# A fused window-attention and gated-FFN kernel: longer warm-up matmuls, one tile in two token parts, one copy on the vector engine, earlier final waits, and one add on GpSimd

## Chip, cores and metric

The kernel runs on one NeuronCore of one Trainium2 chip. The metric is the device time of one execution in microseconds (us), the median of several. The profile's span (first to last recorded instruction) is 1.7 to 2.4 us shorter than that time.

Names used: PE is the matmul engine, PEld its weight loads, DVE the vector engine, ACT the scalar engine, POOL GpSimd, SP SyncE, which here only issues transfers. A "q" after a name (POOLq) is that engine's instruction sequencer. "ps" is PSUM.

## The reference, cut to what matters

```python
def reference(A_x, A_wqkv, A_wo, B_x, B_w_gate, B_w_up, B_w_down):
    x = A_x                                   # 1 x 2048 x 576, bf16
    xn = layernorm(x)
    s = window_attention(xn, A_wqkv, A_wo)    # 32 heads of 18, each query sees the last 256 keys
    h = sigmoid(xn @ B_w_gate) * (xn @ B_w_up)   # 576 -> 4608
    return x + s * silu(h @ B_w_down)         # B_x is not used
```

## The kernel before

The 2048 tokens go through in four chunks of 512. The program is a graph of operations that a list scheduler, inside the kernel, puts in order for each engine before anything is emitted. A change in one place can therefore move instructions elsewhere. These are the parts that the change touches (cuts are marked):

```python
NWARM = 60
PARTS = ((0, 1), (1, 2), (2, 4))      # token blocks of 128 in which gate/up tiles 0-2 of chunk 0 are computed

# build_consts: matmuls on zeros, which keep PE active until the first real work is there
zero = self.hT[:, 0, 0:2 * P]                        # 256 columns
z = op("DVE", 600, lambda e: e.memset(zero, 0.0), "init:zero", prio=0)
...
for i in range(NWARM):                               # each is a pair of 64-row matmuls
    ... pair(eng, self.halves(h, 2 * P), lambda r, t: zero[r, 0:P], lambda r, t: zero[r, :], True, True)

# build_ln, chunk 0: the first 64 columns of the normalised row are written twice
dup = op("POOL", 260, lambda e, ...: e.tensor_scalar(self.xnr[:, sn, 0:RD], x_in[:, 0:RD], ..., ALU.subtract, ALU.mult), ...)

# attention: spreading the queries to the padded layout, 160 transfers issued by GpSimd
o = self.dma(dst, src, ..., f"dma:sp:{c}:{u}:{w}:{gi}", ("qk", par, gi), deps=[ev, war, self.op_qz], prio=1, eng="POOL")

# build_final: the last steps of a token block (t = tanh part, s_ = attention, xf = x)
q2 = op("DVE", ..., lambda e: e.scalar_tensor_tensor(t, t, 1.0, s_, ALU.add, ALU.mult), ...)
q3 = op("DVE", dve_ns(w, 2.0), lambda e: e.tensor_tensor(xf, xf, t, ALU.add), f"fq3:{nm}", deps=[q2, o_dx], prio=2)
# then: out[rows] <- xf, from SyncE. The last block is done in 384 + 192 columns, with one store.

# run_engine: after its last store SyncE waits for every transfer lane
if e == "SP":
    for i, n in enumerate(lane_cnt):
        if n > 0:
            eng.wait_ge(lanes[i], n)
    eng.nop()
...
with nc.Block() as block:             # each engine's program; all meet at the block's end
```

The softmax here doesn't subtract the row's maximum and nothing guards it: scores larger than these inputs give would overflow.

## Time and profile before

| | before |
|---|---|
| time, median of the first 3 runs | 579.93 us (579.84 to 580.57) |
| span of the profile | 578.4 us |
| first real gate/up matmul starts | 8.49 us |
| tile 3 (first full-width tile) starts | 16.49 us |
| last matmul starts | 573.51 us |
| last store issued, seen landed | 575.26, 577.05 us |

First the page's table of busy times (busy us, share of the span, instructions), and its summary of the chain that ended last:

```profile
PE 569.9 (99%) x9542; PEld 362.2 (63%) x9542; DVE 345.5 (60%) x837; ACT 267.8 (46%) x379; POOL 179.9 (31%) x290
...
PE 97%; DVE 2%; issue 1%; ACT 0%; POOL 0%; DVEq 0%
```

PE is all that matters between the first real matmul and the last; only the two ends are open to a change like this one. The timeline of the start (columns: start us, duration us, engine, source line, operation, output<-input, shape, count, and in brackets the idle time before it and what ended it):

```profile
5.03 0.74 POOL L500 TENSOR_SCALAR xnr<-x,small 128x64 bf16<-128x64 bf16 x1
...
5.91 0.32 PE L550 MATMUL ps<-ident,xnr 64*128 64x64 bf16 x10
...
9.31 0.43 DVE L493 TENSOR_SCALAR xnr<-x,small 128x576 bf16<-128x576 bf16 x1 [0.85 <-POOL small L488]
9.38 0.73 POOL L500 TENSOR_SCALAR xnr<-x,small 128x64 bf16<-128x64 bf16 x1
...
10.26 0.32 PE L550 MATMUL ps<-ident,xnr 64*128 64x64 bf16 x10 [0.16 <-DVE small L465]
...
12.73 0.21 PE L98 MATMUL ps<-xnT,wgs 64*128 64x128 bf16 x1 [0.92 <-issue]
...
16.49 0.39 PE L98 MATMUL ps<-xnT,wgr 64*128 64x512 bf16 x2
```

L550 is a transpose of a normalised block. The first and the last of them wait for GpSimd's copy (L500, 0.73 us). For the last the view names a memset of the vector engine (L465) instead; in the code no transpose depends on it, and the copy had ended at 10.11, shortly before. At 12.73 one matmul comes 0.92 us late ("issue": it waits for nothing that the profile shows); from the start of the one ahead of it, at 11.60, to its own it is 1.14 us.

The tail, from the same view:

```profile
573.67 0.36 DVE L1004 TENSOR_TENSOR xf<-xf,thf 128x384 bf16<-128x384 bf16 x1
...
573.95 0.60 DVE L994 TENSOR_TENSOR s_attn<-s_attn,ps 128x96 bf16<-128x96 bf16 x2
...
574.98 0.26 DVE L1004 TENSOR_TENSOR xf<-xf,thf 128x192 bf16<-128x192 bf16 x1
575.26 0.34 SPq L254 DMA_DIRECT2D out_dram<-xf  x1
```

The last view: the instructions that belong to two source lines, the final wait loop (L1151) and the block (L1154). Its columns are line, sequencer, operation, count, shortest/median/longest duration in ns, first and last start in us:

```profile
L1151 SPq EVENT_SEMAPHORE  x28: 17/28/28, 575.7 to 577.9; - x28
```

SyncE's 28 waits start some 61 ns apart, with one gap at the lane of the last store: 15 of them come only after it has landed.

### The profile page before, as it was taken

How to read it: one execution, taken by the hardware profiler on the slowest of the kernel's cores; microseconds unless marked ns; L12 is line 12 of the kernel's file. 1: busy time of each engine (PE TensorE's matmuls, PEld its weight loads, DVE VectorE, ACT ScalarE, POOL GpSimd, SP SyncE). 2: the span in 40 equal slices, each digit the busy share in tenths (PEclk: the TensorE clock that was granted, in tenths of full speed). 3: DMA queues.
4: the chain of work that ended last, by engine and by line, in shares of the span. 5: the costliest groups of instructions: out<-in, count | busy, mean ns of one | idle time of the engine just before them, and what ended most of it. 6: DMA issues, size and time to landing. Idle time of an engine off the chain costs nothing.

```text
span 578.4 us, 21485 instructions
## 1 busy us (share of the span) xinstructions
PE 569.9 (99%) x9542; PEld 362.2 (63%) x9542; DVE 345.5 (60%) x837; ACT 267.8 (46%) x379; POOL 179.9 (31%) x290
## 2 busy tenths in 40 slices
PE   8999999999999999999999999999999999999996
PEld 7555455678985556555788875555457754444786
DVE  4478989845899775577876578877321133333123
ACT  2247568421676653856663566685221023232111
POOL 7466454107564443145534354340000000000000
PEclk9999999999999999999999999999999999999999
DMA  8978865922313433333611023343340015442010
GB/s 241 272 200 202 223 188 159 213 46 55 90 51 95 133 94 110 93 92 96 116 36 43 19 57 105 108 119 111 114 144 22 23 58 152 132 141 74 2 43 23
DMA packets 104908, 62.06 MB, mean 107 GB/s; under 512 B 15308, under 2 KB 103452, under 8 KB 104816
## 3 DMA queue, kind: packets, MB, share of 16 engines
q1 hardware_dynamic: 99696, 55.95, 35.4%
q0 software_dynamic: 5120, 4.74, 3.3%
q8 instruction: 75, 1.23, 0.9%
q14 instruction: 17, 0.14, 0.1%
HBM read 51.61 MB, written 2.36 MB: 93 GB/s over the span
## 4 chain that ended last, share of the span: by engine, by line
PE 97%; DVE 2%; issue 1%; ACT 0%; POOL 0%; DVEq 0%
PE ps L98 96%; DVE hT L890 1%; PE ps L550 1%; ACT tring L887 0%; DVE pvs L767 0%; DVE s_attn L994 0%; DVE thf L999 0%; DVE xf L1004 0%; POOL small L488 0%; DVE expr L714 0%; DVE xnr L493 0%; DVE small L465 0%; DVE pvs L771 0%; DVE hT L418 0%; DVE small L486 0%
## 5 line engine op out<-in xcount | busy, mean ns | idle before, releaser
L98 PE MATMUL ps<-xnT,wgs 64*128 64x512 bf16 (+2 forms) x2400 | 288.4, 368 | 1.0 <-issue 0.9
L98 PEld LDWEIGHTS ps<-xnT,wgs 64*128 64x128 bf16 x2400 | 111.7, 94 | 113.7 <-PE ps L98 1.6
L701 ACT ACTIVATE expr<-ps 128x1024 bf16<-128x1024 f32 (+2 forms) x160 | 156.2, 983 | 52.1 <-PE ps L98 51.6
L98 PE MATMUL ps<-wd_sb,hT 64*128 64x288 bf16 (+2 forms) x2448 | 154.9, 276 | 0.0
L887 ACT ACTIVATE tring<-ps 128x512 bf16<-128x512 f32 x144 | 85.7, 596 | 130.4 <-PE ps L98 128.0
L890 DVE SCALAR_TENSOR_TENSOR hT<-tring,ps 128x512 bf16<-128x512 bf16 x144 | 98.5, 685 | 79.4 <-ACT tring L887 77.3
L98 PEld LDWEIGHTS ps<-wd_sb,hT 64*128 64x128 bf16 x2448 | 118.0, 94 | 22.3
L254 POOL DMA_DIRECT2D qk<-qd x160 | 82.2, 523 | 86.6 <-DVE qd L588 48.7
L666 POOL TENSOR_SCALAR kx<-kprev,small 128x256 bf16<-128x256 bf16 x64 | 64.8, 1023 | 72.1 <-PE ps L98 71.7
L714 DVE TENSOR_TENSOR expr<-expr,mask 128x256 bf16<-128x256 bf16 (+2 forms) x232 | 64.9, 301 | 29.8 <-ACT expr L701 28.4
L767 DVE TENSOR_REDUCE pvs<-ps 64x304 f32<-64x608 f32 x64 | 50.4, 787 | 17.5 <-PE ps L98 16.3
L98 PE MATMUL ps<-qk,kx 64*128 64x320 bf16 (+4 forms) x736 | 59.9, 251 | 0.0
L98 PE MATMUL ps<-xnT,wgr 64*128 64x512 bf16 (+2 forms) x300 | 55.9, 368 | 1.4 <-DVE hT L890 1.2
L98 PEld LDWEIGHTS ps<-qk,kx 64*128 64x128 bf16 x736 | 31.7, 94 | 25.2 <-ACT expr L701 1.7
L984 ACT ACTIVATE thf<-ps 128x576 bf16<-128x576 f32 (+3 forms) x22 | 11.4, 519 | 70.1 <-PE ps L98 69.5
L98 PEld LDWEIGHTS ps<-v_aug,expr 64*128 64x128 bf16 x2432 | 35.5, 93 | 6.2 <-issue 0.2
L98 PE MATMUL ps<-v_aug,expr 64*128 64x19 bf16 (+1 forms) x2432 | 35.9, 170 | 0.0
L98 PE MATMUL ps<-xnT,wqk 64*128 64x512 bf16 x256 | 32.0, 376 | 0.0
L588 DVE CAST qd<-ps 128x1024 bf16<-128x1024 f32 (+1 forms) x20 | 22.1, 1116 | 7.7 <-PE ps L98 7.5
L666 DVE TENSOR_SCALAR kx<-qk,small 128x512 bf16<-128x512 bf16 x64 | 23.5, 388 | 5.3 <-DMA qk<-qd 4.6
L987 DVE SCALAR_TENSOR_TENSOR thf<-thf,ps 128x576 bf16<-128x576 bf16 x12 | 9.1, 754 | 29.3 <-ACT thf L984 28.7
L98 PEld LDWEIGHTS ps<-xnT,wgr 64*128 64x128 bf16 x300 | 14.9, 94 | 15.4 <-DVE hT L890 3.4
(66 smaller groups left out, 293.8 us busy)
## 6 DMA issues: line engine op xcount, KB each, us to landing
wgs<-in_B_w_gate_dram SPq DMA_DIRECT2D x72, 256.0 KB, 3.1
wgs<-in_B_w_up_dram SPq DMA_DIRECT2D x72, 256.0 KB, 3.5
wd_sb<-in_B_w_down_dram SPq DMA_DIRECT2D x9, 576.0 KB, 4.9
qk<-qd POOLq DMA_DIRECT2D x100, 36.0 KB, 2.0
xf<-in_A_x_dram SPq DMA_DIRECT2D x16, 144.0 KB, 2.8
out_dram<-xf SPq DMA_DIRECT2D x16, 144.0 KB, 1.8
xr<-in_A_x_dram SPq DMA_DIRECT2D x6, 288.0 KB, 3.8
wqk<-in_A_wqkv_dram SPq DMA_DIRECT2D x2, 576.0 KB, 6.6
```

The costliest lines, as they stand in the source:

```text
L98: res = eng.matmul(outs[i], lhs(ROWS[t], i), rhs(ROWS[t], i), start=start, stop=stop, tile_position=(64 * t, 0))
L254: o = self.op(eng, DMA_ISSUE_NS[eng], lambda e: e.dma_start(dst, src), name, deps, prio, nbytes=nbytes)
L550: res = eng.transpose(self.psb[:, o:o + 64], src(r, k * P), self.ident[r, :], tile_position=(64 * t, 0))
L588: return eng.tensor_copy(dst, self.both(h, n))
L666: return e.tensor_scalar(self.kx[:, sx, pos:pos + n_ // SW, t, :], src.rearrange("p (s k) -> p s k", k=SW), self.half[:, t:t + 1], None, A ...
L701: return eng.activation(self.expr[:, se, :, lo * SW:NT], self.both(h, NT)[:, :, lo * SW:NT], ACTF.Exp, scale=SM_SCALE)
L714: return eng.tensor_tensor(e_, e_, m_, ALU.mult)
L767: return eng.tensor_reduce(out[ROWS[i]], src, mybir.AxisListType.X, ALU.add)
L887: th = op("ACT", act_ns(NT), lambda e: e.activation(self.tring[:, st, :], bank(h, 0), ACTF.Tanh, scale=0.5), f"th:{c}:{ft}", deps=[pg, dt_ ...
L890: mu = op("DVE", dve_ns(NT), lambda e: e.scalar_tensor_tensor(self.hT[:, ft, :], self.tring[:, st, :], 1.0, bank(h, 1), ALU.add, ALU.mult) ...
L984: return e.activation(v2(t)[:, a:b, :], y2()[:, a:b, :], ACTF.Tanh, scale=0.25)
L987: q1 = op("DVE", dve_ns(w), lambda e: e.scalar_tensor_tensor(v2(t), v2(t), 1.0, y2(), ALU.add, ALU.mult), f"fq1:{nm}", deps=[th, f2], prio=0)
```

## The change

The intent: warm-ups of the full 512 columns, so that fewer instructions keep PE as active; the early gate/up tiles done one after the other, with tile 2 in two token parts and not three; the copy of 64 columns on the vector engine; SyncE's waits in its idle time ahead of the last store; and the 384-column add of the last block off the vector engine, which has the tail's chain to itself then.

```diff
-NWARM = 60
-PARTS = ((0, 1), (1, 2), (2, 4))
+NWARM = 36
+PARTS = (((0, 1), (1, 2), (2, 4)), ((0, 1), (1, 2), (2, 4)), ((0, 2), (2, 4)))
...
-        zero = self.hT[:, 0, 0:2 * P]
+        zero = self.hT[:, 0, :]
...
-                return pair(eng, self.halves(h, 2 * P), ...)
-            w = op("PE", 220 if i < 18 else 110, f_warm, ...)
+                return pair(eng, self.halves(h, NT), ...)
+            w = op("PE", 432 if i < 9 else 216, f_warm, ...)
... # layer-norm of chunk 0: the copy goes from POOL's tensor_scalar to DVE's tensor_copy
... # early tiles: loop over tiles outside, over their parts inside
-        q3 = op("DVE", dve_ns(w, 2.0), lambda e: e.tensor_tensor(xf, xf, t, ALU.add), f"fq3:{nm}", deps=[q2, o_dx], prio=2)
+        big = w < D and c0 == 0
+        q3 = op("POOL" if big else "DVE", 700 if big else dve_ns(w, 2.0), lambda e: e.tensor_tensor(xf, xf, t, ALU.add), f"fq3:{nm}",
+                deps=[q2, o_dx], prio=2)
...
+                if e == "SP" and o is self.prog[e][-1]:
+                    for i, n in enumerate(lane_cnt):
+                        if n > 0 and i not in outs:
+                            eng.wait_ge(lanes[i], n)
...
             if e == "SP":
-                for i, n in enumerate(lane_cnt):
-                    if n > 0:
-                        eng.wait_ge(lanes[i], n)
+                for i in outs:
+                    eng.wait_ge(lanes[i], lane_cnt[i])
                 eng.nop()
```

`big` is true for one operation only, the add of the first 384 columns of the last token block.

More of the change, by code (lines that the diff above doesn't have):

```diff
@@ L55 @@
 NTAIL = 96
-NWARM = 60
-PARTS = ((0, 1), (1, 2), (2, 4))
+NWARM = 36
+PARTS = (((0, 1), (1, 2), (2, 4)), ((0, 1), (1, 2), (2, 4)), ((0, 2), (2, 4)))
+XPRIO = 0
 NQK = 5
@@ L381, in load_x @@
             for i in range(BPC):
-                self.x_dma[i] = (self.dma(self.x0[:, i, :], self.x[i * P:(i + 1) * P, :], P * D * 2, f"dma:x{i}", ("x0", i), prio=0),
+                self.x_dma[i] = (self.dma(self.x0[:, i, :], self.x[i * P:(i + 1) * P, :], P * D * 2, f"dma:x{i}", ("x0", i), prio=XPRIO * (i > 1)),
                                  self.x0[:, i, :])
@@ L424, in f_warm @@
             def f_warm(eng):
-                return pair(eng, self.halves(h, 2 * P), lambda r, t: zero[r, 0:P], lambda r, t: zero[r, :], True, True)
-            w = op("PE", 220 if i < 18 else 110, f_warm, f"warm:{i}", deps=[z], prio=4, acq=None if i else h, odeps=[w])
+                return pair(eng, self.halves(h, NT), lambda r, t: zero[r, 0:P], lambda r, t: zero[r, :], True, True)
+            w = op("PE", 432 if i < 9 else 216, f_warm, f"warm:{i}", deps=[z], prio=4, acq=None if i else h, odeps=[w])
             w.filler = h
@@ L495, in build_ln @@
                 ALU.subtract, ALU.mult), f"ln:ap:{st}", deps=[rs, ag, dn], prio=pr)
-            if c:
-                dup = op("DVE", 180, lambda e, sn=sn: e.tensor_copy(self.xnr[:, sn, 0:RD], self.xnr[:, sn, RD:2 * RD]),
-                         f"ln:dup:{st}", deps=[ap], prio=pr)
-            else:
-                dup = op("POOL", 260, lambda e, ss=ss, x_in=x_in, sn=sn: e.tensor_scalar(
-                    self.xnr[:, sn, 0:RD], x_in[:, 0:RD], self.mv[:, ss, 0:1], self.rstd[:, ss, :],
-                    ALU.subtract, ALU.mult), f"ln:dup:{st}", deps=[rs, ag, dn], prio=pr)
+            dup = op("DVE", 180, lambda e, sn=sn: e.tensor_copy(self.xnr[:, sn, 0:RD], self.xnr[:, sn, RD:2 * RD]),
+                     f"ln:dup:{st}", deps=[ap], prio=pr)
             if c:
@@ L505, in build_ln @@
             self.r_st.release(ss, ap)
-            self.r_st.release(ss, dup)
             if c:
@@ L869, in gate_up @@
             sw, fc = slots[ft // WG], slice((ft % WG) * P, (ft % WG + 1) * P)
-            b0, b1 = (0, BPC) if part is None else PARTS[part]
+            b0, b1 = (0, BPC) if part is None else PARTS[ft][part]
             t0, n = b0 * P, (b1 - b0) * P
@@ L901, in build_ffn @@
             hs = [self.pool_f.hold() for _ in range(2)] + [self.pool_s.hold()]
-            his = [None] * early
-            for part in range(len(PARTS)):
-                los = [gate_up(ft, hs[ft], 0, None if part else hs[ft], part, [his[ft]]) for ft in range(early)]
-                for ft in range(early):
-                    u = his[ft] = gate_up(ft, hs[ft], 1, None, part, [los[ft]])
-                    if part == len(PARTS) - 1:
-                        tail(ft, hs[ft], u)
-                    if part == len(PARTS) - 1 and ft == 1:
-                        self.r_w.release(slots[0], u)
+            for ft, h in enumerate(hs):
+                u = None
+                for part in range(len(PARTS[ft])):
+                    lo = gate_up(ft, h, 0, None if part else h, part, [u])
+                    u = gate_up(ft, h, 1, None, part, [lo])
+                tail(ft, h, u)
+                if ft == 1:
+                    self.r_w.release(slots[0], u)
         for ft in range(early, NFT):
@@ L1127, in emit @@
                     o.tok = (("E", e), cnt[e])
+        outs = [i for lane, i in self.lane_ids.items() if lane[0] == "out"]
         def semof(key):
```

## The prediction

> **What bounds the kernel.** TensorE. The table of busy times has PE at 569.9 of 578.4 us (99%), and the chain of work that ended last is 97% PE. From 12.7 us to 573.7 us PE has only a dozen gaps of 0.2 to 0.9 us. So nothing can be won in the middle; the change works on the first 16.5 us and on what follows the last matmul (573.7 us).
>
> **The start (timeline, 0 to 17 us).** The first real matmuls wait for layer-norm, then the transposes. Before: 24 pairs of 256-column warm-ups until 5.8, transpose 0 at 5.91, first gate matmul at 8.49. PE then idles twice: 0.3 us at 9.9 (transpose 3 waits for GpSimd's copy, 0.73 us, ended 10.11), and 1.1 us at 11.6, where a matmul that waits for no semaphore comes late. I read this second one as the instruction stream: an instruction packet of 16 KB starts at 10.33 in the DMA records, and PE resumes at 12.73 with its 450th instruction.
>
> After:
> - Warm-ups are 15 + 7 + 3 pairs of 512 columns. Cold pairs cost 427 ns (2 x 213 measured), warm ones 218 (2 x 109). The clock rose 3.8 us after the first warm-up, which agrees with about 3.4 us in the Trainium skill ("TensorE: Matmul & The Clock Gate", Part 1). The first block then ends near 6.4, not 5.8; first gate matmul near 8.9: +0.4 us.
> - The copy moves to DVE (about 0.1 us): transpose 3 no longer waits: -0.3.
> - PE issues 80 fewer instructions before the gates and longer ones after, so the 450th comes near 14.5 while its packet should be there by 14.2: -1.0 to -1.1.
> - Waiting for the last transpose's evictions may cost 0.2 again; tile 2 in two parts saves 0.03 of matmul time.
>
> Net: tile 3's first matmul moves from 16.49 to about 15.4-15.6: -1.0 us (my range -1.3 to -0.1). Weights for later tiles land 3 us or more ahead of use, so the gain should last.
>
> **The end.** The last store is issued at 575.26 and has landed by 577.05. The list of SyncE instructions shows 29 semaphore waits after its issue, 61 ns each; 13 are hidden in the flight, but 15 stand after the out lane's wait and end at 578.0. Put ahead of the store they fall into SyncE's idle time (570.4 to 575.2): -0.9 to -1.0 us.
>
> The 384-column add leaves DVE (0.36 us at 573.67), so the tail's first multiply can start about 0.18 us earlier. On GpSimd it takes an estimated 0.9 us (2.6 cycles per element, "GPSIMD Engine Reference", section 3.1, plus start-up; here a 256-column copy takes 0.43), ending near 574.7, ahead of DVE's last add (575.05). It may slow DVE's last operations: -0.1 (range -0.2 to +0.3).
>
> **Middle.** The scheduler reorders some rows; work is equal: 0 +- 0.5 us.
>
> **Sum.** -1.0 - 0.95 - 0.1 = -2.1 us: **577.8 us**, 8-in-10 range 576.7 to 579.2. Faster by over 2%: 0.005; within 2%: 0.99; slower: 0.005.
>
> **Right or wrong by:** the first gate matmul at about 8.9; no PE gap near 11.6; tile 3 at about 15.5; 29 waits before the last store, and about 1.0 us (not 2.0) less between landing and end; GpSimd's add 0.7 to 1.1 us, off the chain.
>
> **What would make it wrong:** the instruction stall only moves, to where PE is again ahead of its packet; warm-ups of 512 columns shift the clock's rise; GpSimd's add becomes the last thing the store waits for; new gaps in the middle from the changed order, which can each be 0.3 to 0.9 us.

## More of the kernel before

```profile
L1154 POOLq DRAIN  x1: 8982/8982/8982, 389.6 to 389.6; - x1
L1154 PEldq DRAIN  x1: 658/658/658, 573.1 to 573.1; - x1
L1154 ACTq DRAIN  x1: 281/281/281, 574.2 to 574.2; - x1
L1154 DVEq DRAIN  x1: 297/297/297, 575.0 to 575.0; - x1
...
L1154 SPq DRAIN  x1: 13/13/13, 578.2 to 578.2; - x1
```

The DRAIN lines are each engine's own end of the block. GpSimd's is 8.98 us long and starts at 389.6 us, because GpSimd has nothing left to do from there on. It costs nothing there, and it is counted in no engine's busy time.

## The result, and the profile after

The changed kernel is slower: 583.92 us (583.38 to 584.12, 4 runs), before 580.25 us (579.84 to 580.60, 4 runs). The ratio is 1.0062 (95% interval 1.0045 to 1.0079). Ratios here and below are the mean time of one kernel's fast runs over that of the other's in the same rounds, so not quite the ratio of the medians quoted. The outputs are correct.

Busy times and chain after:

```profile
PE 569.1 (98%) x9484; PEld 351.3 (60%) x9484; DVE 346.7 (60%) x840; ACT 268.8 (46%) x379; POOL 175.6 (30%) x287
...
PE 96%; DVE 1%; ACT 1%; issue 1%; DVEq 0%
```

PE does a little less and the span is 3.4 us longer, so time is added where PE stands still. It is not at the start:

```profile
6.13 0.31 PE L545 MATMUL ps<-ident,xnr 64*128 64x64 bf16 x10
...
9.33 1.12 DVE L494 TENSOR_SCALAR xnr<-x,small 128x576 bf16<-128x576 bf16 x1 [0.23 <-PE ps L99]
9.36 0.93 POOL L451 MEMSET v_aug<- 128x192 bf16 x1
...
11.19 0.32 PE L545 MATMUL ps<-ident,xnr 64*128 64x64 bf16 x10
...
12.31 0.28 PE L99 MATMUL ps<-xnT,wgr 64*128 64x256 bf16 x2
...
15.50 0.38 PE L99 MATMUL ps<-xnT,wgr 64*128 64x512 bf16 x2
```

Tile 3 starts at 15.50, as predicted; the late matmul of before is gone. (The vector engine's normalisation of the last block took 1.12 us here, where it took 0.43 before. It ran beside a GpSimd memset. PE was not ready for that block any sooner, so this did no harm.)

The tail is better too:

```profile
572.09 0.91 POOL L999 TENSOR_TENSOR xf<-xf,thf 128x384 bf16<-128x384 bf16 x1 [189.54 <-DVE thf L993]
...
572.18 0.61 DVE L988 TENSOR_TENSOR s_attn<-s_attn,ps 128x96 bf16<-128x96 bf16 x2 [0.18 <-PE ps L99]
...
573.24 0.26 DVE L999 TENSOR_TENSOR xf<-xf,thf 128x192 bf16<-128x192 bf16 x1
573.59 0.34 SPq L255 DMA_DIRECT2D out_dram<-xf  x1
```

The store is issued 1.67 us earlier than before, and GpSimd's add is over (573.00) before the vector engine's last one begins. The loss is behind it. The waits of SyncE in the last 12 us (who waited for whom, us in total, times, longest):

```profile
SPq L1155 <- PEq L1155: 6.2, 1, 6.2
SPq L1146 <- POOL xf L999: 2.6, 1, 2.6
SPq L1153 <- DMA out_dram<-xf: 1.4, 1, 1.4
SPq L1146 <- DVE xf L999: 0.5, 1, 0.5
```

(L1146 is the wait for what the last store needs: it waits for GpSimd's add, and then 0.5 us more for the vector engine's.)

The instructions of the moved waits (L1136), of the wait for the last store (L1153) and of the block (L1155), with columns as before, one fence each:

```profile
L1136 SPq EVENT_SEMAPHORE  x27: 17/28/28, 568.8 to 570.4; - x27
```

```profile
L1153 SPq EVENT_SEMAPHORE  x1: 17/17/17, 575.4 to 575.4; - x1
```

```profile
L1155 POOLq EVENT_SEMAPHORE  x2: 17/17/17, 581.6 to 581.7; - x2
...
L1155 POOLq DRAIN  x1: 9532/9532/9532, 572.0 to 572.0; - x1
...
L1155 SPq DRAIN  x1: 13/13/13, 575.6 to 575.6; - x1
L1155 SPq EVENT_SEMAPHORE  x1: 17/17/17, 581.7 to 581.7; - x1
```

The 27 waits are in SyncE's idle time now. SyncE is done at 575.6 and then stands for 6.2 us at the block's meeting point. The first line names PEq as the releaser; this is the case that the view's own warning is about, for PE had been done for 9 us. The one that came last is GpSimd: its DRAIN runs from 572.04 to 581.58. The add that keeps GpSimd busy until 573.00 has moved the start of that drain from 389.6 to 572.0, and nothing hides it there. The chain of work that ended last does not show this either: it ends with the vector engine's last add, since a drain is not counted as work.

The two spans add up as follows, in us. In the row "landed to the end", 1.37 is the rest of SyncE's waits and the meeting of the engines, and 6.42 is the drain with the meeting behind it.

| stretch | before | after | difference |
|---|---|---|---|
| start to tile 3 | 16.49 | 15.50 | -0.99 |
| tile 3 to the last matmul | 557.02 | 556.44 | -0.58 |
| last matmul to the last store's issue | 1.75 | 1.65 | -0.10 |
| issue to landed, as SyncE sees it | 1.79 | 1.79 | 0 |
| landed to the end | 1.37 | 6.42 | +5.05 |
| span | 578.42 | 581.80 | +3.38 |

### The profile page after: what moved, and what is told of

Its sections match the earlier page's. It is cut to its first block, busy times and chain, and to the rows that moved or that the text cites. A ratio compares the mean times of both kernels' runs of the same rounds, so it can differ in the third digit from the quotient of the medians.

```text
span 581.8 us, 21366 instructions
## 1 busy us (share of the span) xinstructions
PE 569.1 (98%) x9484; PEld 351.3 (60%) x9484; DVE 346.7 (60%) x840; ACT 268.8 (46%) x379; POOL 175.6 (30%) x287
## 3 DMA queue, kind: packets, MB, share of 16 engines
q0 software_dynamic: 5120, 4.74, 3.3%
## 4 chain that ended last, share of the span: by engine, by line
PE 96%; DVE 1%; ACT 1%; issue 1%; DVEq 0%
PE ps L99 96%; DVE hT L885 1%; PE ps L545 1%; ACT tring L882 0%; ACT expr L696 0%; ACT xnT L522 0%; DVE s_attn L988 0%; DVE thf L993 0%; DVE hT L419 0%; DVE xf L999 0%; DVE small L487 0%; DVE small L410 0%; DVE expr L709 0%; DVEq L1146 0%
## 5 line engine op out<-in xcount | busy, mean ns | idle before, releaser
L99 PEld LDWEIGHTS ps<-wd_sb,hT 64*128 64x128 bf16 x2448 | 112.5, 94 | 27.3
L661 POOL TENSOR_SCALAR kx<-kprev,small 128x256 bf16<-128x256 bf16 x64 | 63.4, 999 | 53.0 <-PE ps L99 52.3
```

What stands on the lines that cost most here:

```text
L99: res = eng.matmul(outs[i], lhs(ROWS[t], i), rhs(ROWS[t], i), start=start, stop=stop, tile_position=(64 * t, 0))
L661: return e.tensor_scalar(self.kx[:, sx, pos:pos + n_ // SW, t, :], src.rearrange("p (s k) -> p s k", k=SW), self.half[:, t:t + 1], None, A ...
```

## The experiments

Theory A: the loss is GpSimd's drain, which begins after its last instruction. Rival B: it is the new order of work or the lower mean clock (0.994 against 1.0). Rival C: it is the store's wait for the slow add.

### e1_add_on_dve, e2_only_add, e3_after_no_drain, e4_late_memset

e1 is the changed kernel with the add back on the vector engine. e2 is the kernel before with the add alone moved. e3 is the changed kernel whose block is told to end without GpSimd's drain. e4 is the kernel before with a late GpSimd instruction that nobody waits for.

```diff
# e1, on the changed kernel
-        big = w < D and c0 == 0
+        big = False
# e2, on the kernel before: the q3/big lines of the change, nothing else
# e3, on the changed kernel
-        with nc.Block() as block:
+        with nc.Block(no_gpsimd_drain=True) as block:
# e4, on the kernel before, after q3
+        if w < D and c0 == 0:
+            op("POOL", 150, lambda e: e.memset(self.kprev[:, 0, 0:64], 0.0), "late", deps=[q2, list(self.op_kp.values())], prio=9)
```

> The changed kernel with its last 384-column add put back on the vector engine, all else kept. Theory A (the GpSimd drain at the block's end, 9.5 us long, now starts at 572.0 and is the last thing to end): the drain goes back to about 390 us, the span ends with SyncE's wait near 575.6 plus 0.2, so about 575.9 span and 577.3 to 577.8 us measured, 2.3 to 3.0 us under the kernel before. Rival B (the loss comes from the new order of work or from the lower mean clock, 0.994): stays within 1 us of 583.9.

> The kernel before with only the 384-column add moved to GpSimd. Theory A: GpSimd's last instruction starts at 573.7, its drain ends about 9.5 us later at 583.2, the span is about 583.4 (before 578.4) and the time about 585.2, 5 us slower than before. Rival B: within 0.5 us of before. Rival C (the store waits for a slow GpSimd add): at most 0.5 us slower, and the store issued later than 575.3.

> The changed kernel, add on GpSimd, but the block closes without GpSimd's drain. Theory A: no long GpSimd DRAIN in the trace, end about 0.2 us after SyncE's last wait at 575.4, span about 575.7, time 577.2 to 577.7. Rival B: stays at about 583.9. Result must stay correct.

> The kernel before plus one small GpSimd memset (64 columns of a buffer nobody reads any more) after the last block's product, near 573.7; nothing waits for it. Theory A: any late GpSimd instruction exposes the drain: ends about 9 us after it, near 582.7 to 583.2, about 4.5 to 5 us slower than before. Rival C (only the add counts, since the store waits for it): no change, within 0.3 us.

| run | time, us (range) | ratio to before (95%) | landed to end, us |
|---|---|---|---|
| before | 580.61 (579.92 to 581.18) | | 1.37 |
| e1 | 578.19 (577.95 to 578.44) | 0.9959 (0.9944 to 0.9974) | 0.46 |
| e2 | 585.61 (585.21 to 586.44) | 1.0089 (1.0074 to 1.0104) | 6.43 |
| e3 | 579.01 (577.67 to 579.68) | 0.9970 (0.9954 to 0.9987) | 0.52 |
| e4 | 584.86 (583.91 to 587.67) | 1.0086 (1.0055 to 1.0117) | 5.58 |

GpSimd's drain in the instructions of the block, first e1, then e2, then e4:

```profile
L1155 POOLq DRAIN  x1: 8969/8969/8969, 382.6 to 382.6; - x1
```

```profile
L1156 POOLq DRAIN  x1: 9527/9527/9527, 574.9 to 574.9; - x1
```

```profile
L1156 POOLq DRAIN  x1: 8732/8732/8732, 573.9 to 573.9; - x1
```

Theory A holds in all four, and both rivals fall. (e1's time is 0.4 us above the range expected of it, e4's loss 0.25 us below.) With the add on the vector engine everything else of the change is worth 2.4 us. The add alone costs 5.0 us. A memset of 0.15 us that nobody waits for costs 4.3 us, so the wait for the add is not it; in e2 the store is issued 1.69 us after the last matmul starts, and before it was 1.75. Nor is it the clock: in the trace of after the granted clock is 1.00 from 20 to 573 us and 0.50 from 576 us on, so the lower mean comes of the idle end. In e3 the trace has no DRAIN of GpSimd at the block's end, and the add on GpSimd does no harm. The DRAIN record starts about when the last instruction does and covers it; from the end of that instruction to the end of the drain it is 8.56 to 8.58 us in every one of before, after, e1, e2 and e4.

e3 came out above what was expected of it (577.2 to 577.7). Its profile shows why one run can: PE's clock rose only at about 7.1 us there, against 5.0 in e1, and tile 3 began at 16.75 us. This happens in all kernels (see below). e2's profile caught a late rise too (6.8), and its late matmul came 2.02 us after the one ahead of it, not 1.14; its last matmul is 1.2 us later than before's.

### e5_add_block14: does the place of the last instruction count?

```diff
# on the changed kernel
-        big = w < D and c0 == 0
+        big = sb == NC * BPC - 2
... # and the scheduler's estimate for the add on GpSimd: 1000 ns for 700
```

> The changed kernel, but GpSimd takes the whole add (576 columns) of the second-last token block instead of the last block's 384 columns. Theory A1 (the drain ends 8.57 us after the end of GpSimd's last instruction, measured 8.56 to 8.58 in five runs so far, wherever that is): the add starts near 568, lasts about 1.3 us, so the drain ends near 578 and the span is about 578.2, 2 us over the version with both adds on the vector engine (576.4). Rival A2 (what is exposed is tied to the last block's add): span about 576.

```profile
L1155 POOLq DRAIN  x1: 9901/9901/9901, 568.5 to 568.5; - x1
```

One execution, 580.66 us, span 578.6. The add (576 columns) started at 568.55 and took 1.28 us, the drain ended at 578.40, 8.58 us after it; the store had landed at 576.05. A1 holds. An instruction on GpSimd is free here only if it ends some 8.6 us ahead of everything else.

### e6_no_pool_dma, e9_half_dma, e10_few_dma, e13_quarter_dma, e14_last_half_dma: what makes the drain long?

All five are the changed kernel, late add on GpSimd, with some or all of GpSimd's 160 transfers issued from SyncE's queue instead. (A first form of e9 and e10, in which both queues signalled one semaphore, was refused before it was submitted, by the author's account; the record does not hold it. Each queue has its own semaphores in what ran.)

```diff
-                o = self.dma(..., ("qk", par, gi), deps=[ev, war, self.op_qz], prio=1, eng="POOL")
# e6: all from SyncE
+                o = self.dma(..., ("qk", par, gi), deps=[ev, war, self.op_qz], prio=1, eng="SP")
# e9 (M = "c < 2"), e10 (M = "c == 0 and u == 0 and gi == 0"), e13 (M = "c < 1"), e14 (M = "c >= 2"); c is the chunk
+                o = self.dma(..., ("qk", par, gi, M), deps=[ev, war, self.op_qz], prio=1, eng="POOL" if M else "SP")
```

> The changed kernel, but the 160 transfers that GpSimd issues (queries to their padded layout) are issued from SyncE's queue; the late add stays on GpSimd. Theory D1 (the drain is long because GpSimd has issued DMAs in software): the GpSimd DRAIN falls to under 1 us. Rival D2 (a fixed price of the GpSimd drain): again 8.5 to 8.6 us after the add's end. The time may rise or fall, since SyncE's queue takes 160 more issues; only the drain's length counts.

> The changed kernel with the query transfers of the first two of four chunks (half of 160) issued by GpSimd, the rest by SyncE. The last transfer that GpSimd issues is then about 300 us ahead of its last add. If the drain's length goes with the number of transfers GpSimd has issued: about 4.3 us. If it is a fixed price once GpSimd has issued any: 8.5 to 8.6 us after the add's end. If it goes with transfers still under way: near 0 (but that was already unlikely, since before's drain came with the last of them long landed).

> As the run with half of them, but only one transfer is left to GpSimd. Proportional: drain about 0.1 us after the add. Fixed: 8.5 to 8.6 us.

> The changed kernel, late add on GpSimd, with only the first chunk's 40 query transfers issued by GpSimd. If the number counts, with a bend between 80 and 160: about 3.3 us from the add's end to the drain's end (half of 6.62). If the age of the last transfer counts: a little below 6.62 us, 5 to 6.5.

> The same with the 80 transfers of the last two chunks. If the number counts: again 6.6 us. If the age of the last one counts: 8.6 us, as with all 160.

The add took 0.91 us in each, and the DRAIN record covers it. The drains of e6, e13, e9 and e14, one fence each:

```profile
L1155 POOLq DRAIN  x1: 1017/1017/1017, 574.8 to 574.8; - x1
```

```profile
L1155 POOLq DRAIN  x1: 4304/4304/4304, 573.9 to 573.9; - x1
```

```profile
L1155 POOLq DRAIN  x1: 7571/7571/7571, 571.3 to 571.3; - x1
```

```profile
L1155 POOLq DRAIN  x1: 7571/7571/7571, 573.9 to 573.9; - x1
```

| transfers issued by GpSimd | run | end of the add to end of the drain, us |
|---|---|---|
| 0 | e6 | 0.07 |
| 1 | e10 | 0.16 |
| 40, the first ones | e13 | 3.35 |
| 80, the first ones | e9 | 6.62 |
| 80, the last ones | e14 | 6.62 |
| 160 | after | 8.58 |

The drain is the price of the transfers that GpSimd has issued. It goes with their number, 0.08 us each up to 80 ((6.62 - 0.07) / 80), and not with how long ago they were: in these runs the last was issued at 382 us or earlier, 190 us and more ahead of the drain, and the first 80 cost what the last 80 cost. The record cannot tell the number of transfers from what grows in step with it: each transfer is 32 packets, 40 of them make 1280 packets and 1.18 MB, 160 make 5120 and 4.74 MB. Between 80 and 160 the growth bends. Neither of the two laws written down for e9 fits alone, and what sets the bend is open.

These kernels are no better than the changed one with the add on the vector engine: 580.17 us (e13), 580.69 (e6), 580.85 (e9), 581.28 (e10) and 583.81 (e14), one execution each.

### e7_waits_only and e8_front_only: what are the other parts worth?

e7 is the kernel before with only the moved waits. e8 is the changed kernel with the waits and the add as before.

```diff
# e7, on the kernel before: the wait lines of the change, nothing else
# e8, on the changed kernel: big = False, and the waits back behind the last store
```

> The kernel before with only the waits moved ahead of the last store. From the trace of before: 15 waits of 61 ns after the landing disappear, so landing to end falls by 0.9 to 1.0 us, time 0.9 to 1.0 us less than before (ratio about 0.9984). Rival: the waits were hidden in any case, no change.

> The changed kernel with the waits and the last add as before: only the front (512-column warm-ups, tile 2 in two parts, copies on the vector engine) and the order of work that follows from it. As predicted: tile 3 starts near 15.5 instead of 16.5 us, the 1.1 us gap at 11.6 is gone, time 1.0 us less than before (ratio about 0.998), more if the middle has also fewer gaps (the changed kernel's last matmul came 1.57 us earlier). Rival: no gain, since the rise of the clock moves by as much.

e7: 579.43 us (578.66 to 582.83) against 580.26 (579.64 to 582.72), ratio 0.9992 (0.9972 to 1.0012). The times alone do not show a gain; one run on each side (582.83 and 582.72) lies over 1.5 us above the others. The trace does: landed to end is 0.46 us and was 1.37, while the last matmul starts at 573.51 in both. So the waits are worth 0.91 us.

e8: 579.54 us (578.09 to 579.82), ratio 0.9985 (0.9972 to 0.9997). In its profile tile 3 starts at 15.26 us and the last matmul at 571.43, 2.1 us earlier than before.

### e11_warm_only and e12_parts_dup: which part of the front?

e11 is the kernel before with the warm-up lines of the change only. e12 is e8 with the warm-ups of before, so it has only the copies on the vector engine, tile 2 in two parts and the early tiles one after the other.

> The kernel before with only the warm-ups of 512 columns. If the gap of 1.1 us at 11.6 us was the instruction stream, and its place is counted in instructions: with 80 fewer instructions in front it comes some 80 instructions later in the work, where matmuls have 256 columns, and shrinks below 0.4 us; the wait of 0.3 us for the last copy on GpSimd stays. Time 0.5 to 1 us less than before. Rival (the gap is a wait for a transfer or an eviction that the trace does not show): it stays near the same matmul, about 1 us long.

> The kernel before with the copies on the vector engine and tile 2 in two parts, warm-ups as before. Instruction theory: still a gap of about 1 us without a semaphore, again near TensorE's 450th instruction; the wait for the last transposed tile goes. Time 0 to 0.4 us less than before. Rival: the gap is gone, since the order around it changed.

e11 missed its time: 580.70 us (579.71 to 582.10), ratio 1.0007 (0.9988 to 1.0027). The gap did what the instruction theory says. It stands again between the 449th and the 450th instruction of PE, now 0.32 us and not 1.14 from one matmul to the next, at 13.26 us, ahead of a matmul of 256 columns, and tile 3 starts at 15.60 us. But from tile 3 to the last matmul it takes 557.66 us, where before took 557.02, and a gap of 0.79 us at 284.7 us is new:

```profile
285.51 0.66 PE L98 MATMUL ps<-wd_sb,hT 64*128 64x288 bf16 x8 [0.50 <-issue]
```

This one gap is the whole loss. Up to it the matmuls come in the order of before, and just ahead of it they are 0.16 us earlier than before, counted from tile 3; right behind it they are 0.62 us later, and at the end 0.64. What the front won, the middle lost.

The kept traces say more of these gaps than the experiments do. In all 17 traces, from 10 us on, PE has five waits of over 0.15 us that the profile puts down to nothing ("issue"): at the 450th instruction in the four kernels with before's front (before, e2, e4, e7), and this one. The start of PE's next instruction follows the start of a 16 KB packet of instructions each time (us):

| run | packet starts | PE goes on | difference |
|---|---|---|---|
| before | 10.33 | 12.73 | 2.4 |
| e2 | 11.26 | 13.87 | 2.6 |
| e4 | 10.62 | 13.12 | 2.5 |
| e7 | 10.35 | 12.88 | 2.5 |
| e11, the new gap | 282.98 | 285.51 | 2.5 |

e2, whose packet came latest of the four, has the longest wait:

```profile
13.87 0.21 PE L98 MATMUL ps<-xnT,wgs 64*128 64x128 bf16 x1 [1.81 <-issue]
```

So the gaps go with the arrival of instructions, and with fewer warm-up instructions one of them came at another place. That is strong support and no proof, for no run changed the packets themselves.

e12 gained more than expected: 578.98 us (578.25 to 579.26) against 580.35 (580.10 to 583.75), ratio 0.9972 (0.9956 to 0.9989). Tile 3 starts at 16.22 us, only 0.27 earlier, but the middle takes 556.29 us. For the instruction theory it decides nothing. PE has a gap before the 450th instruction is reached, and that one is a wait for a transfer (timeline of PE):

```profile
9.86 0.63 PE L99 MATMUL ps<-xnT,wgs 64*128 64x128 bf16 x16
11.36 0.28 PE L99 MATMUL ps<-xnT,wgr 64*128 64x256 bf16 x2 [0.87 <-DMA wgs<-in_B_w_up_dram]
```

The packet of instructions arrived in its shadow: it started at 8.79 us, not at 10.33.

Two things come out of all these profiles together. First, the middle follows the order of work. Four profiles with before's order (before, e2, e4, e7) took 556.87 to 557.07 us from tile 3 to the last matmul; five with the changed order (after, e1, e3, e8 and e12) took 556.16 to 556.67. So the reordering is worth about 0.6 us. Second, the rise of PE's clock wanders from run to run. The warm-ups start at 1.15 us (256 columns) or 1.28 us (512), and the spacing of the pairs falls to about half at 3.9 us in e12, 4.2 in e8, 4.6 in after, 5.0 in before, 5.9 in e5, 6.8 in e2 and 7.1 in e3. Between e8 and e3 that is 2.9 us, and tile 3 comes 1.5 us later. It is a part of the spread of 1 to 2 us in the times, and no run shows that longer warm-ups bring the rise forward.

### e15_half_dma_add_dve: a faster kernel

> The run with the first 80 on GpSimd, but with the last add on the vector engine. Its last matmul came at 571.15, 1.2 us ahead of the version with all transfers on GpSimd and the add on the vector engine; so the span should be about 575.2, 576.5 to 577.5 us measured, against 578.2 for that version. If the earlier last matmul was an accident of that one run: about 578.

```diff
# on e9
-        big = w < D and c0 == 0
+        big = False
```

577.60 us (577.21 to 577.64) against 580.66 (580.12 to 581.05), ratio 0.9946 (0.9929 to 0.9963), although the clock rose late in the profiled run (6.7 us). From tile 3 to the last matmul it takes 555.26 us (e9: 555.16), about 1 us less than with all transfers on GpSimd. The time is 0.1 us above the range expected. Why the mix of queues shortens the middle was not taken apart. GpSimd's drain, at 386.3 us, is hidden. It beats both kernels. Against e1 (0.9959) the intervals overlap, so that of these two e15 is the better one is not shown by the times.

## Why the prediction was wrong, point by point

- **The end, the step that failed.** The prediction's sum for the end was "-0.9 to -1.0 us" for the waits and "-0.1 (range -0.2 to +0.3)" for the add. Its worries about the add were that it "may slow DVE's last operations" and "becomes the last thing the store waits for". It took SyncE's waits for all that lies between the store and the end. In their place the runs showed a further condition: every engine must have drained, and GpSimd's drain lasts 8.57 us after its last instruction in this program. That put +5.96 us on the end (6.42 - 0.46), and 2.6 us of gains turned into a loss of 3.4 us in the span. The 8982 ns were in the profile of before, in the lines of the block; nothing in the views of busy time, waits or chain points there.
- **The add itself: right.** "An estimated 0.9 us" from the GPSIMD page: 0.91 us measured. The tail's first multiply started 0.24 us after the start of the last matmul and not 0.43, and last matmul to store fell by 0.10 us. Theory C, that the store would wait for it last, did not come true.
- **The waits: right.** 0.91 us, by e7's trace. (The prediction counted 29 waits; the trace has 28.)
- **The start: right in size, not proved in its mechanism.** Predicted tile 3 at "15.4-15.6": 15.50. First gate matmul predicted near 8.9: 8.58, since the clock rose at 4.6 us. The wait for the last transpose's evictions cost 0.4 us and not 0.2. That the missing 1.1 us was the instruction stream is supported by e11 (the same 450th instruction, a different matmul) and by the five waits that end 2.4 to 2.6 us after a packet starts, but no run tested it directly; e12 tested nothing of it. Its fear that "the instruction stall only moves" came true in e11, not in the changed kernel.
- **The middle: just outside the range given** (0 +- 0.5 predicted, -0.58 measured), to the good side, and not zero: the new order is worth about 0.6 us in every profile that has it and all transfers on GpSimd. (The prediction read "a dozen gaps" of PE in before; the trace shows six of over 0.15 us from 12.7 us on.)
- Without the drain the prediction would have held: the changed kernel without it (e3) is at 579.01 us, inside the range 576.7 to 579.2, and with the add back on the vector engine (e1) at 578.19, predicted 577.8.

## What to carry to other kernels

Before giving an engine work near the end of a program, look at what that engine still has to do after its last instruction. Read the records of the block's end and not only busy time and the chain: an engine that finished early may hide microseconds there. On GpSimd that has issued transfers, a last instruction is free only if it ends well (here 8.6 us) ahead of all else; issue the transfers from another queue, or leave GpSimd alone at the end. The first has its own price: with all transfers on SyncE's queue (e6, one execution) the middle took 557.98 us, in the changed kernel 556.44. e3 left the drain out and its outputs were correct, but no run here shows that this is safe in general. And a gain that is read from a trace at both ends should be summed to the very last record, the meeting of the engines included.

## What the Trainium skill lacked or had wrong

- No page that I found tells of GpSimd's drain at the end of a program or what it costs. The runs show 0.07 us with no transfers issued by GpSimd, 0.16 with 1, 3.35 with 40, 6.62 with 80 and 8.57 with 160, counted from the end of its last instruction. It belongs to "GPSIMD Engine Reference" (section 7, pitfalls).
- "VectorE: DVE Perf Modes", section "The DRAIN you can't avoid", tells of two kinds of DRAIN: the flush after each vector operation, and boilerplate of about 12 ns on all five engines. The DRAIN at the block's end fits neither, SyncE's apart (13 ns): it is 658 ns on PE, 281 on ACT, 297 on DVE and 8982 on GpSimd.
- "TensorE: Matmul & The Clock Gate", Part 1, gives about 4 us of activity until the clock rises, +-500 ns between runs (and says that the phase differs by run). Here it rose between 2.7 and 5.9 us after the first warm-up (at 3.9 us in e12, about 7.1 in e3), a wider spread than the page's.
- A stall for the instruction stream in code without a branch belongs to "Runtime: NRT & Kernel Launch", section "Instruction fetch mechanics": it calls the cost of crossing a block of instructions mostly hidden, and has a stall only for a taken branch. PE's records here show no branch, and five of its waits, 0.50 to 1.81 us, each ended 2.4 to 2.6 us after a packet of 16 KB of instructions had started. That the packet was the cause is inferred.
- Agreeing in part: "SBUF — State Buffer", section "SBUF: two separate sides", states an exclusive lock of the port pair that the vector engine and GpSimd share; who starts first has it for the whole instruction. In the 12 traces in which the normalisation of the last block ran beside a GpSimd memset of 0.93 us it took 1.00 to 1.13 us, in the other 5 it took 0.43. But in after the normalisation's record starts first (9.33 us, the memset's at 9.36) and it is still the one that was held up, by 0.69 us and not 0.93. No run shows what passed between the two, nor that this vector instruction is one that needs the shared pair.
